# One PSUM tile for seven banks, and transposes without use in the tensor engine's early gaps

## The chip, the cores and the metric

The kernel runs on one core of a Trainium2 chip. The metric is the device time of one execution in microseconds (us); the time of before is the median of three executions. A profile is one execution recorded by the hardware profiler. Its engines are PE (the tensor engine's matmuls; PEld is its weight loads), DVE (the vector engine), ACT (the scalar engine), POOL (GpSimd) and SP (the queue that issues DMAs).

## The reference

Pre-layernorm attention with one key and value head, then a gated feed-forward layer, on 2048 tokens of width 512, all in fp32:

```python
def A(x, wq, wk, wv, wo):                      # 32 heads of 16, one k and one v
    q = (x @ wq).reshape(B, S, 32, 16).transpose(0, 2, 1, 3)
    p = softmax(einsum("bhqd,bkd->bhqk", q, x @ wk) * 16 ** -0.5)
    return einsum("bhqk,bkd->bhqd", p, x @ wv)...reshape(B, S, 512) @ wo
def Bf(x, W_gate, W_up, W_down):               # width 512 -> 1792 -> 512
    gate, up = x @ W_gate, x @ W_up
    return (gate * (gate > 0) * up) @ W_down
h = x + A(layernorm(x), wq, wk, wv, wo)
out = h + Bf(layernorm(h), W_gate, W_up, W_down)
```

## The kernel before

Matrices are split into a rounded part and a rest (fp32r), and a product is three matmul passes. Attention is cut into 32 units of 2048 query rows by 32 key steps (STEPS). For each of two row halves of the array (rows 0 to 63 and 64 to 127, which can compute beside each other) a step has two kinds of work:

- a **max matmul** (`max_mm`, L619): 512 columns of scores into one PSUM bank, of which DVE takes the row maxima (L621, one TENSOR_REDUCE of 128x512);
- a **score matmul** (`score_mm`, L658): 512 columns of scores, turned so that keys are on the partitions, of which ACT takes the exponential into SBUF (L661).

Two score steps feed one **value block** (`value_block`, L674): four matmuls of 32 columns each into a PSUM bank of its own, named O. The projections and the feed-forward layer are **chains** (`Chain`): accumulations of many passes into one bank, cut into two halves, one for each row half of the array (L297); at the end of a chain ACT (L861, L867) or DVE (L893, L822) reads the bank.

PSUM has eight banks. One is O. The other seven, BANKS = B0 to B6, are handed out by `bank(tag)`: each call makes a new tile of 128x512 fp32 with the bank's name and one buffer, so the next writer of B3 is made to wait for the last reader of B3. The framework adds all waits by itself, from which instruction writes and reads which tile.

What stands after what on every engine is written out by hand: ORDER is a row of 11,274 letters, read one at a time. m and M are a max matmul (lower and upper row half), e and E a score matmul, g and G one pass of a chain's lower or upper half, O a value block, T a set of transposes. The planner only chooses the bank (the free one that it thinks is earliest) and places work that the letters don't name. The row has 2048 m and M, 2048 e and E, 6648 g and G, 512 O and 18 T. The 512 O stand in 336 runs: 214 of one O, 89 of two, and 33 of three to five. 204 runs follow directly on an m, M, e or E. The first O is the 335th letter; `on_` counts the value blocks done. The chains of the row end in 186 readings: 16 query groups, 16 residuals, 98 gate products and 56 partial down products. After the last letter, `run(feed(NT - 1, True))` computes the last tile's feed-forward layer with whole chains (L288).

Of the kernel before, what the change touches and what calls it, by code (L numbers as in the profile page):

```python
# [16 lines left out]
S, D, H, DH, F = 2048, 512, 32, 16, 1792  # L17
# [9 lines left out]
STEPS = NB * 2  # L27
NP = 10
BANKS = [f"B{i}" for i in range(7)]
# [8 lines left out]
PASS, LOAD, SEEN, CHANGE, VALUE, BACK, TURN = 230, 107, 425, 95, 882, 237, 214  # L38

EXP, EXP_FREE, RED, RED_FREE, COPY, ADD, FREE = 494, 650, 600, 740, 541, 600, 150  # L40
ROUND, DIFF, PRODUCT, SCALE, HOP, ISSUE = 640, 1290, 1150, 640, 2600, 600
APPLY, LANDING, ASKED, SPREAD, RAW_LAG = 705, 4700, 5500, 5600, 1500


A_AT, V_AT, P_AT, QUERIES_AT, KEYS_AT, LN_AT = 1800, 1500, 3900, 0, 0, (0, 3000, 2500)

# [110 lines left out]
def block_kernel(ctx: ExitStack, tc: tile.TileContext, x, wq, wkv, wo, wgu, wd, out):  # L157
    nc = tc.nc
    pool = lambda name, **kw: ctx.enter_context(tc.tile_pool(name=name, bufs=1, **kw))
    consts = pool("consts")  # L160
    sb = pool("sb")
    ps = pool("ps", space=PSUM)
# [3 lines left out]
    ident = consts.tile([128, 128], F32, name="ident")  # L166
# [7 lines left out]
    kaug = consts.tile([128, S], F32R, name="kaug")  # L174
# [11 lines left out]


    rota = {"n": 0, "tags": []}

    def bank(tag=None):  # L190
        if tag is None:
            tag = rota["tags"][rota["n"] % len(rota["tags"])]
            rota["n"] += 1
        return ps.tile([128, 512], F32, name=tag, bufs=1)


    clk = {"A": 0.0, "V": 0.0, "P": 0.0, "S": 0.0}
    state = {"on": False, "spare": False, "now": 0.0}
    later, stamp = [], {}
    count = iter(range(1 << 30))  # L200

    def on(engine, t, ns):

        clk[engine] = max(clk[engine], t) + ns
        return clk[engine]

    def at(t, fn):

        if state["on"]:
# [376 lines left out]
    qaug = {}  # L586
# [21 lines left out]

    mpart = {}

    def max_mm(m, ab, tag):

        v, i = divmod(m, STEPS)
        j, p, c = i // 8, i // 4 % 2, i % 4
        if v not in mpart:
            mpart[v] = sb.tile([128, 2, 2, 4, 4], F32, name="mpart", bufs=2)
        r = slice(64 * ab, 64 * ab + 62)
        b = bank(tag)
        nc.tensor.matmul(b, qaug[v][r, p, c * 128:(c + 1) * 128], kaug[r, j * 512:(j + 1) * 512],  # L619
                         start=True, stop=True)  # L620
        nc.vector.tensor_reduce(mpart[v][:, ab, p, c, j:j + 1], b, axis=AX.X, op=ALU.max)  # L621

    def max_finish(v):

        m = sb.tile([128, 2, 8], F32, name="mfin", bufs=2)
        nc.vector.tensor_reduce(m.rearrange("p a n -> p (a n)"), mpart.pop(v).rearrange("p a q c j -> p (a q c) j"),
                                axis=AX.X, op=ALU.max)

        ms = sb.tile([128, 2, 2, 8], F32, name="msplit", bufs=2)
        nc.vector.tensor_copy(ms[:, :, 0].bitcast(F32R), m)  # L630
        nc.vector.tensor_tensor(ms[:, :, 1], m, ms[:, :, 0], op=ALU.subtract)

        mt = sb.tile([128, 32], F32, name="mturned", bufs=2)
        nc.vector.transpose(mt, ms.rearrange("p a l n -> p (a l n)"))
        t = on("V", 0.0, 950) + FREE

        def written():
            nc.sync.dma_start(out=c_dram[v], in_=mt)

        def landed():  # L640
            for ab in range(2):
                nc.sync.dma_start(out=qaug[v][64 * ab + 62:64 * ab + 64].bitcast(F32)
                                  .rearrange("l q (c i j) -> l (q c) i j", i=4, j=32),
                                  in_=c_dram[v].rearrange("(i a l n) j -> a l n i j", i=4, a=2, l=2)[ab])
            stamp["rows", v] = t + 2 * HOP

        at(t, written)
        at(t + HOP, landed)

    probs = {}  # L650

    def score_mm(g, ab, tag):

        v, i = divmod(g, STEPS)
        kb, p = divmod(i, 2)
        r = slice(64 * ab, 64 * ab + 64)
        b = bank(tag)
        nc.tensor.matmul(b, kaug[r, kb * 128:(kb + 1) * 128], qaug[v][r, p, :], start=True, stop=True)  # L658
        if g not in probs:
            probs[g] = sb.tile([128, 2, T], F32, name="p", bufs=NP)  # L660
        nc.scalar.activation(probs[g][:, ab], b, AF.Exp, scale=DH ** -0.5)  # L661

    obank, osb = {}, {}

# [242 lines left out]
    N = len(UNITS) * STEPS  # L907
# [16 lines left out]
    warm = bank("O")  # L924
# [108 lines left out]
    lanes = [0.0, 0.0]  # L1033
    issued = 0.0
    bfree = {tag: 0.0 for tag in BANKS + ["O"]}
    bfree.update(B0=V_AT, B6=V_AT - 200)
    free = list(BANKS)
    ge, me, on_ = [0, 0], [0, 0], 0
    exps, oend, qtime = {}, {}, {0: QUERIES_AT}
    maxed, loaded = 0, 1  # L1040
# [2 lines left out]
    clk.update(A=A_AT, V=V_AT, P=P_AT, S=0.0)  # L1043
    stamp.update({("xnT", 0, k): 0.0 for k in range(KT)})
    stamp["key", 0], stamp["ln", 1] = KEYS_AT, LN_AT[0]
    end_o, end_t = None, False

    def normalise(t):
# [127 lines left out]
    while not done():  # L1176
# [33 lines left out]
        tag = next_bank() if free else None  # L1210
        starts = {}
        for k in range(2):
            g, w, c = ge[k], me[k], (low, high)[k]
            if g < N and ("rows", g // STEPS) in stamp and g - NP < 2 * on_ and tag:
                starts["eE"[k]] = place(k, max(stamp["rows", g // STEPS], bfree[tag]))
            if w < N and w // STEPS in qtime and w // STEPS <= maxed + 1 and tag and (
                    w >= STEPS or ("key", w // 8) in stamp):
                starts["mM"[k]] = place(k, max(qtime[w // STEPS], bfree[tag], stamp["key", w // 8] if w < STEPS else 0.0))
            if c is not None and (c.tag or tag):
                starts["gG"[k]] = place(k, max(c.t, 0.0 if c.tag else bfree[tag]) if c.i == 0 else 0.0)  # L1220
        top = max(lanes)
        if on_ < N // 2 and len(exps.get(2 * on_ + 1, ())) == 2:
            dep = max(max(exps[g].values()) for g in range(2 * on_, 2 * on_ + 2)) + FREE
# [26 lines left out]
        if any(x.ready() + CHANGE <= top and (x.ready() + 4000 < top or on_ == N // 2) for x in turns):  # L1250
            do_turns()
            continue
        letter = next(order)
        if letter == "T":
            if pending in turns:
                turns.remove(pending)
            for source in (fronts, feeds):
                if source.held is pending:
                    source.held = None
            turn_now(pending, tag, False, end_t)  # L1260
            continue
        kind, k = letter.upper(), int(letter.isupper())
        issued = s = starts[letter]
        end_t = False
        if kind != "O":
            end_o = None
        if kind == "O":
            value_block(on_)
            v, i = divmod(on_, NB)
            end_o = s + VALUE  # L1270
            lanes = [end_o + BACK] * 2
            issued = end_o - 400
# [80 lines left out]
```

## Time and profile before

| | |
|---|---|
| median of three executions | 1734.67 us (1733.37 to 1734.95) |
| the profiled execution | 1735.53 us, span 1733.8 us from its first to its last instruction |
| mean granted clock of PE | 0.994 |

The profile's page has the busy time of each engine, the chain of waits that ended last, and groups of instructions by line with their mean duration and the idle time before them. The view by time (timeline) lists start, duration, engine, line, operation and count; a bracket gives the idle time before an instruction and what ended it. The view by windows gives, for a stretch of time, its length, then busy time and number of instructions of PE, PEld, DVE, ACT and POOL, then the granted clock of PE (1.00 is full speed), the DMA share and GB/s. Instructions of PE are pipelined, so a busy PE is not one at its peak.

### The profile page before, as it was taken

The page shows a single profiled execution, that of the slowest core. Times are in us where ns is not written, and L with a number is a line of the kernel's source. Part 1 is how long each engine was busy: PE and PEld are TensorE (multiplying, and loading weights), DVE is VectorE, ACT ScalarE, POOL GpSimd, SP SyncE. Part 2 cuts the span into 40 slices and gives each one's busy share as a digit, 9 for nine tenths or more (in the row PEclk, how much of TensorE's full clock was granted, in tenths as well). Part 3 has the DMA queues.
Part 4 walks back from the last instruction along what each step waited for, and adds up shares of the span by engine and source line. Part 5 has one row for each costly group of instructions (what it writes and reads, how often), then busy time and mean ns, then how long its engine had stood idle before and what let it go on. Part 6 is the DMA issues. An engine that isn't in the chain of part 4 may idle for free.

```text
span 1733.8 us, 40138 instructions
## 1 busy us (share of the span) xinstructions
PE 1712.0 (99%) x15566; PEld 1141.9 (66%) x15566; DVE 1451.0 (84%) x2524; ACT 1251.2 (72%) x2488; POOL 854.0 (49%) x1015
## 2 busy tenths in 40 slices
PE   8999999999999999999999999999999999999999
PEld 6755334766656666666766667666666666666688
DVE  8899999988998888988888888897898888986266
ACT  7478977777777777777777777777767777778724
POOL 5511301666415656286544667276655557276410
PEclk9999999999999999999999999999999999999999
DMA  3323211332212222233222223232223223122343
GB/s 129 92 74 86 77 32 26 97 95 79 83 58 72 75 79 81 71 96 97 77 61 83 77 87 99 72 103 70 79 69 108 77 79 102 48 87 81 107 138 116
DMA packets 101970, 144.07 MB, mean 83 GB/s; under 512 B 27156, under 2 KB 39572, under 8 KB 101780
## 3 DMA queue, kind: packets, MB, share of 16 engines
q1 hardware_dynamic: 100724, 141.19, 27.4%
q8 instruction: 122, 2.00, 0.5%
q14 instruction: 68, 0.56, 0.1%
q10 hardware_dynamic: 1056, 0.33, 0.1%
HBM read 119.73 MB, written 21.49 MB: 81 GB/s over the span
## 4 chain that ended last, share of the span: by engine, by line
PE 93%; DVE 5%; issue 1%; DMA 1%; ACT 0%; POOL 0%; SPq 0%; POOLq 0%; DVEq 0%; ACTq 0%
PE B L297 27%; PE O L674 27%; PE B L658 16%; PE B L619 16%; PE B L288 4%; DVE mpart L621 4%; PE B L514 1%; PE O L926 1%; PE B L404 0%; DVE msplit L630 0%; PE B L1001 0%; DMA c_dram<-mturned 0%; DVE hn L397 0%; DMA qaug<-c_dram 0%; PE B L581 0%
## 5 line engine op out<-in xcount | busy, mean ns | idle before, releaser
L621 DVE TENSOR_REDUCE mpart<-B 128x1 f32<-128x512 f32 x2048 | 1268.8, 682 | 190.6 <-PE B L619 111.6
L661 ACT ACTIVATE p<-B 128x512 f32<-128x512 f32 x2048 | 1091.0, 606 | 359.8 <-PE B L658 200.3
L619 PE MATMUL B<-kaug,qaug 62*128 62x512 f32 x2048 | 746.6, 421 | 8.3 <-DVE hT L566 2.6
L658 PE MATMUL B<-qaug,kaug 64*128 64x512 f32 x2048 | 713.6, 417 | 5.6 <-DMA qaug<-c_dram 3.6
L297 PE MATMUL B<-hn,gu 64*128 64x256 f32 x4704 | 564.8, 282 | 0.0
L297 PEld LDWEIGHTS B<-hn,gu 64*128 64x128 f32 x4704 | 533.9, 186 | 24.6 <-issue 15.6
L674 PE MATMUL O<-p,vv 128*32 128x512 f32 x4096 | 510.4, 601 | 0.0
L619 PEld LDWEIGHTS B<-kaug,qaug 62*128 62x128 f32 x2048 | 348.3, 185 | 157.7 <-DVE mpart L621 52.7
L658 PEld LDWEIGHTS B<-qaug,kaug 64*128 64x128 f32 x2048 | 337.6, 186 | 164.7 <-DVE mpart L621 53.4
L869 POOL TENSOR_TENSOR hf<-hf,ga 128x256 f32<-128x256 f32 x92 | 67.4, 733 | 426.0 <-ACT hf L867 417.7
L297 PE MATMUL B<-wd,hT 64*128 64x512 f32 x1176 | 274.6, 395 | 0.1
L240 POOL TENSOR_TENSOR gu<-wraw,gu 128x512 fp32r<-128x512 f32 x195 | 252.9, 1297 | 16.3
L674 PEld LDWEIGHTS O<-p,vv 128*32 128x32 f32 x4096 | 99.8, 109 | 192.0 <-issue 175.5
L297 PEld LDWEIGHTS B<-wd,hT 64*128 64x128 f32 x1176 | 192.0, 185 | 15.3 <-issue 2.7
L240 POOL TENSOR_TENSOR wd<-wraw,wd 128x512 fp32r<-128x512 f32 x95 | 122.4, 1289 | 7.9
L239 POOL TENSOR_SCALAR gu<-wraw 128x512 fp32r<-128x512 f32 x195 | 120.8, 619 | 11.1 <-PE B L297 8.0
L297 PE MATMUL B<-wo,act 64*128 64x512 f32 x384 | 88.3, 394 | 0.1
L240 POOL TENSOR_TENSOR hT<-hf,hT 128x256 fp32r<-128x256 f32 x97 | 72.9, 752 | 8.1
L357 POOL TENSOR_TENSOR rs<-ve,nhalf 128x2 f32<-128x2 f32 (+1 forms) x13 | 10.2, 783 | 125.5 <-DVE nm L353 125.4
L861 ACT ACTIVATE ga<-B 128x256 f32<-128x256 f32 x112 | 43.5, 388 | 39.0 <-PE B L288 24.6
L297 PEld LDWEIGHTS B<-wo,act 64*128 64x128 f32 x384 | 62.6, 185 | 5.5 <-issue 1.7
L528 POOL TENSOR_TENSOR act<-raw,act 128x512 fp32r<-128x512 f32 x16 | 20.6, 1290 | 89.4 <-ACT raw L527 85.7
(134 smaller groups left out, 916.3 us busy)
## 6 DMA issues: line engine op xcount, KB each, us to landing
wraw<-wgu SPq DMA_DIRECT2D x224, 256.0 KB
wraw<-wd SPq DMA_DIRECT2D x112, 256.0 KB
q_dram<-act SPq DMA_DIRECT2D x32, 256.0 KB
qaug<-q_dram SPq DMA_DIRECT2D x62, 128.0 KB
o_dram<-osb SPq DMA_DIRECT2D x31, 256.0 KB
x<-x SPq DMA_DIRECT2D x16, 256.0 KB
out<-h SPq DMA_DIRECT2D x16, 256.0 KB
qaug<-q_dram SPq DMA_DIRECT2D x62, 64.0 KB
```

Source lines behind the costliest of these rows:

```text
L239: nc.gpsimd.tensor_scalar(dst[:, 0], src, 1.0, 0.0, op0=ALU.mult, op1=ALU.add)
L240: nc.gpsimd.tensor_tensor(dst[:, 1], src, dst[:, 0].bitcast(F32), op=ALU.subtract)
L288: nc.tensor.matmul(out(self.bank), l(a), r(b), start=i == 0, stop=i == len(self.ops) - 1)
L297: mm = nc.tensor.matmul(out(self.bank), l(a)[rows], r(b)[rows], start=opens and which == 0, stop=closes and which == 1)
L528: nc.gpsimd.tensor_tensor(qs[:, 1], q, qs[:, 0].bitcast(F32), op=ALU.subtract)
L619: nc.tensor.matmul(b, qaug[v][r, p, c * 128:(c + 1) * 128], kaug[r, j * 512:(j + 1) * 512], start=True, stop=True)
L621: nc.vector.tensor_reduce(mpart[v][:, ab, p, c, j:j + 1], b, axis=AX.X, op=ALU.max)
L658: nc.tensor.matmul(b, kaug[r, kb * 128:(kb + 1) * 128], qaug[v][r, p, :], start=True, stop=True)
L661: nc.scalar.activation(probs[g][:, ab], b, AF.Exp, scale=DH ** -0.5)
L674: nc.tensor.matmul(obank[v][32 * h:32 * h + 32], vv[:, kb, :], probs[g + p][:, ab], start=kb == 0, stop=kb == NB - 1)
L861: nc.scalar.activation(ga[:, :n], p[:, :n], AF.Relu)
L869: nc.gpsimd.tensor_tensor(hf[:, :n], hf[:, :n], ga[:, :n], op=ALU.mult)
```

## The change

Three things change. The other parts of the diff (the letters X, P and W, `max_mm` and `score_mm` with a pair of banks, POOL_ROWS) are not reached: the row of letters is the same and has none of them, and POOL_ROWS is 0.

```diff
+WARMERS = True
+    banks = ps.tile([128, len(BANKS), 512], F32, name="B", bufs=1)
     def bank(tag=None):
...
-        return ps.tile([128, 512], F32, name=tag, bufs=1)
+        return banks[:, BANKS.index(tag)] if tag in BANKS else ps.tile([128, 512], F32, name=tag, bufs=1)
...
         kind, k = letter.upper(), int(letter.isupper())
+        if on_ == 0 and WARMERS:
+            idle = starts[letter] - max(last_busy, max(lanes) - 6000.0)
+            if idle > 400:
+                warm = bank("O")
+                for _ in range(min(16, int((idle - 200) / 150))):
+                    nc.tensor.transpose(warm[:, :128], ident, ident)
+            last_busy = starts[letter] + PASS
```

First, the seven banks become seven slices of one tile, made once. Second, as long as no value block has been computed, a gap of over 400 ns that the planner expects ahead of a letter gets up to 16 transposes of the identity into bank O. Third, some lines move (L619 is L627 now, L658 is L683, L297 is L303, L674 is L702, L621 is L630, L661 is L687).

The instructions of PE, DVE, ACT and POOL stand in the same order as before, and each uses the same bank, but for the added transposes on PE: 111, in 12 groups. The waits differ. In the order as built, with the engines that a row waits for, PE in the middle of the program stands so before the change (B2 and so on are the bank, the number behind it the tile, qaug and kaug the queries and keys, p the exponentials, wd and hT a chain's operands; the last two rows are the halves of two chains):

```order
L674 MATMUL O_6091<-p_6568,vv_79 32x512 x2
L619 MATMUL B2_6640<-kaug_78,qaug0_75 128x512 [waits DVE_49]
L658 MATMUL B5_6643<-qaug1_76,kaug_78 128x512 [waits Activation_49]
L658 MATMUL B6_6647<-qaug1_76,kaug_78 128x512 [waits Activation_49]
L658 MATMUL B3_6650<-qaug1_76,kaug_78 128x512 [waits DVE_49]
L297 MATMUL B0_6654<-wd_5756,hT_5447 128x512 [waits DVE_49]
L297 MATMUL B1_6590<-wd_5756,hT_5447 128x512 [waits Activation_sequencer_49]
```

Each of these waits is for the last reader of the same bank, which stands several matmuls further up: the score matmul into B6 waits for the exponential that last read B6. The same place of PE with the change (B_87 is the one tile):

```order
L702 MATMUL O_5142<-p_5548,vv_79 32x512 x2
L627 MATMUL B_87<-kaug_78,qaug0_75 128x512
L683 MATMUL B_87<-qaug1_76,kaug_78 128x512 [waits DVE_49]
L683 MATMUL B_87<-qaug1_76,kaug_78 128x512 [waits Activation_49] x2
L303 MATMUL B_87<-wd_4861,hT_4602 128x512 [waits Activation_49]
L303 MATMUL B_87<-wd_4861,hT_4602 128x512 [waits Activation_sequencer_49]
```

No instruction moved; the waits did. The count of the semaphore that each waits for belongs here to the reader of the matmul in the row directly above: the first score matmul waits for the reduction of the max matmul above it, the second for the exponential of the first, the third for that of the second, and the chain's pass for that of the third, though all four write different banks. Over the whole program PE's instructions have 2215 waits for ACT and 2177 for DVE before, 2198 and 2168 with the change. Before, nearly all are for a reader of the bank that is about to be written. With the change, 4351 of the 4366 are for the youngest reader of the tile that stands earlier in the program, whichever bank it reads.

DVE and ACT get waits too: DVE has 104 for ACT before and 1152 now, ACT 36 for DVE before and 940 now. Nearly all name a count that PE has already waited for ahead of the matmul whose result is to be read.

At the start of PE's row, ahead of the first value block, this stood (L581 are transposes of normalised inputs):

```order
L581 MATMUL B1_435<-ident_68,h_89 128x128 [waits Activation_49]
L581 MATMUL B1_435<-ident_68,h_90 128x128 [waits Pool_49] x2
L619 MATMUL B2_442<-kaug_78,qaug0_75 128x512 [waits DVE_49]
L581 MATMUL B3_445<-ident_68,h_89 128x128 [waits PE_49]
L581 MATMUL B3_445<-ident_68,h_89 128x128
```

and now the same place has three added transposes, and the same kind of waits as above:

```order
L587 MATMUL B_87<-ident_68,h_90 128x128 [waits Activation_49]
L587 MATMUL B_87<-ident_68,h_91 128x128 [waits Pool_49] x2
L1314 MATMUL O_433<-ident_68 128x128 [waits PE_49]
L1314 MATMUL O_433<-ident_68 128x128 x2
L627 MATMUL B_87<-kaug_78,qaug0_75 128x512 [waits Activation_49]
L587 MATMUL B_87<-ident_68,h_90 128x128 [waits DVE_49]
L587 MATMUL B_87<-ident_68,h_90 128x128
```

The transposes went in between; the max matmul now waits for ACT's reading of another bank, and the transposes behind it for the max matmul's reduction.

More of the change, by code (lines that the diff above doesn't have):

```diff
@@ L40 @@
 EXP, EXP_FREE, RED, RED_FREE, COPY, ADD, FREE = 494, 650, 600, 740, 541, 600, 150
+EXP_TWO, RED_TWO = 860, 1134
+ROWS_HOP, ROWS_AT = 2600, 5200
+POOL_ROWS = 0
+WARMERS = True
 ROUND, DIFF, PRODUCT, SCALE, HOP, ISSUE = 640, 1290, 1150, 640, 2600, 600
@@ L609, in block_kernel, with max_mm @@
     mpart = {}
-    def max_mm(m, ab, tag):
+    def max_mm(m, ab, tag, pair=None):
         v, i = divmod(m, STEPS)
@@ L616, in max_mm @@
             mpart[v] = sb.tile([128, 2, 2, 4, 4], F32, name="mpart", bufs=2)
[L617 to L621, printed above, removed]
+        for h in (ab, 1 - ab) if pair is not None else (ab,):
+            r = slice(64 * h, 64 * h + 62)
+            b = bank(tag) if pair is None else banks[:, pair + h]
+            nc.tensor.matmul(b, qaug[v][r, p, c * 128:(c + 1) * 128], kaug[r, j * 512:(j + 1) * 512],
+                             start=True, stop=True)
@@ L623, in max_finish @@
+        if pair is None:
+            nc.vector.tensor_reduce(mpart[v][:, ab, p, c, j:j + 1], b, axis=AX.X, op=ALU.max)
+        else:
+            nc.vector.tensor_reduce(mpart[v][:, :, p, c, j], banks[:, pair:pair + 2], axis=AX.X, op=ALU.max)
     def max_finish(v):
         m = sb.tile([128, 2, 8], F32, name="mfin", bufs=2)
-        nc.vector.tensor_reduce(m.rearrange("p a n -> p (a n)"), mpart.pop(v).rearrange("p a q c j -> p (a q c) j"),
-                                axis=AX.X, op=ALU.max)
@@ L629, in max_finish @@
         ms = sb.tile([128, 2, 2, 8], F32, name="msplit", bufs=2)
-        nc.vector.tensor_copy(ms[:, :, 0].bitcast(F32R), m)
-        nc.vector.tensor_tensor(ms[:, :, 1], m, ms[:, :, 0], op=ALU.subtract)
+        part = mpart.pop(v).rearrange("p a q c j -> p (a q c) j")
+        flat = m.rearrange("p a n -> p (a n)")
+        if v < POOL_ROWS:
+            half = sb.tile([128, 16, 2], F32, name="mhalf", bufs=2)
+            nc.gpsimd.tensor_tensor(half, part[:, :, :2], part[:, :, 2:], op=ALU.max)
+            nc.gpsimd.tensor_tensor(flat, half[:, :, 0], half[:, :, 1], op=ALU.max)
+            nc.gpsimd.tensor_scalar(ms[:, :, 0].bitcast(F32R), m, 1.0, None, op0=ALU.mult)
+            nc.gpsimd.tensor_tensor(ms[:, :, 1], m, ms[:, :, 0], op=ALU.subtract)
+            t = on("P", clk["V"] + FREE, 1000) + FREE
+            at(t, lambda: max_turned(v, ms, on("V", t, 250) + FREE))
+        else:
+            nc.vector.tensor_reduce(flat, part, axis=AX.X, op=ALU.max)
+            nc.vector.tensor_copy(ms[:, :, 0].bitcast(F32R), m)
+            nc.vector.tensor_tensor(ms[:, :, 1], m, ms[:, :, 0], op=ALU.subtract)
+            max_turned(v, ms, on("V", 0.0, 950) + FREE)
@@ L633, in max_finish, with max_turned @@
+    def max_turned(v, ms, t):
         mt = sb.tile([128, 32], F32, name="mturned", bufs=2)
         nc.vector.transpose(mt, ms.rearrange("p a l n -> p (a l n)"))
-        t = on("V", 0.0, 950) + FREE
         def written():
@@ L644, in landed, with score_mm @@
                                   in_=c_dram[v].rearrange("(i a l n) j -> a l n i j", i=4, a=2, l=2)[ab])
-            stamp["rows", v] = t + 2 * HOP
+            stamp["rows", v] = t + ROWS_AT
         at(t, written)
-        at(t + HOP, landed)
+        at(t + ROWS_HOP, landed)
     probs = {}
-    def score_mm(g, ab, tag):
+    def score_mm(g, ab, tag, pair=None):
         v, i = divmod(g, STEPS)
         kb, p = divmod(i, 2)
-        r = slice(64 * ab, 64 * ab + 64)
-        b = bank(tag)
-        nc.tensor.matmul(b, kaug[r, kb * 128:(kb + 1) * 128], qaug[v][r, p, :], start=True, stop=True)
+        for h in (ab, 1 - ab) if pair is not None else (ab,):
+            r = slice(64 * h, 64 * h + 64)
+            b = bank(tag) if pair is None else banks[:, pair + h]
+            nc.tensor.matmul(b, kaug[r, kb * 128:(kb + 1) * 128], qaug[v][r, p, :], start=True, stop=True)
         if g not in probs:
             probs[g] = sb.tile([128, 2, T], F32, name="p", bufs=NP)
-        nc.scalar.activation(probs[g][:, ab], b, AF.Exp, scale=DH ** -0.5)
+        if pair is None:
+            nc.scalar.activation(probs[g][:, ab], b, AF.Exp, scale=DH ** -0.5)
+        else:
+            nc.scalar.activation(probs[g], banks[:, pair:pair + 2], AF.Exp, scale=DH ** -0.5)
     obank, osb = {}, {}
@@ L1045, in block_kernel @@
     stamp["key", 0], stamp["ln", 1] = KEYS_AT, LN_AT[0]
+    last_busy = 0.0
     end_o, end_t = None, False
@@ L1220, in block_kernel @@
                 starts["gG"[k]] = place(k, max(c.t, 0.0 if c.tag else bfree[tag]) if c.i == 0 else 0.0)
+        pair = min((i for i in range(len(BANKS) - 1) if BANKS[i] in free and BANKS[i + 1] in free),
+                   key=lambda i: max(bfree[BANKS[i]], bfree[BANKS[i + 1]]), default=None)
+        ahead = int(lanes[0] > lanes[1])
+        if pair is not None:
+            both = max(bfree[BANKS[pair]], bfree[BANKS[pair + 1]])
+            g, w = ge[0], me[0]
+            if ge[0] == ge[1] and g < N and ("rows", g // STEPS) in stamp and g - NP < 2 * on_:
+                starts["X"] = place(ahead, max(stamp["rows", g // STEPS], both))
+            if me[0] == me[1] and w < N and w // STEPS in qtime and w // STEPS <= maxed + 1 and (
+                    w >= STEPS or ("key", w // 8) in stamp):
+                starts["P"] = place(ahead, max(qtime[w // STEPS], both, stamp["key", w // 8] if w < STEPS else 0.0))
         top = max(lanes)
@@ L1253, in block_kernel @@
         letter = next(order)
+        if letter == "W":
+            lanes = [max(l, later[0][0]) for l in lanes]
+            continue
         if letter == "T":
@@ L1262, in block_kernel @@
         kind, k = letter.upper(), int(letter.isupper())
+        if on_ == 0 and WARMERS:
[5 more added lines that the diff above has]
+            last_busy = starts[letter] + PASS
+        if kind in "XP":
+            s = starts[letter]
+            issued = max(lanes[1 - ahead], s)
+            lanes[ahead], lanes[1 - ahead] = s + PASS, issued + PASS
+            end_o, end_t = None, False
+            if kind == "X":
+                score_mm(ge[0], ahead, None, pair)
+                e0 = max(clk["A"], issued + SEEN, oend.get(ge[0] - NP, 0.0))
+                clk["A"] = e0 + EXP_TWO
+                exps[ge[0]] = {0: clk["A"] + 100, 1: clk["A"] + 100}
+                ge = [ge[0] + 1] * 2
+                done_at = e0 + EXP_TWO + 156
+            else:
+                max_mm(me[0], ahead, None, pair)
+                r0 = max(clk["V"], issued + SEEN)
+                clk["V"] = r0 + RED_TWO
+                me = [me[0] + 1] * 2
+                done_at = r0 + RED_TWO + 140
+                if me[0] == (maxed + 1) * STEPS:
+                    max_finish(maxed)
+                    maxed += 1
+            bfree[BANKS[pair]] = bfree[BANKS[pair + 1]] = done_at
+            continue
         issued = s = starts[letter]
```

## The prediction

> **What bounds the kernel now.** I read the page first: span, busy engines, chain of waits.
>
> ```profile
> span 1733.8 us, 40138 instructions
> PE 1712.0 (99%) x15566; PEld 1141.9 (66%) x15566; DVE 1451.0 (84%) x2524; ACT 1251.2 (72%) x2488; POOL 854.0 (49%) x1015
> PE 93%; DVE 5%; issue 1%; DMA 1%; ACT 0%; POOL 0%; SPq 0%; POOLq 0%; DVEq 0%; ACTq 0%
> ```
>
> PE is the bound: 99% busy, and 93% of the chain that ended last. DVE and ACT work beside it. The groups of instructions say what each does:
>
> ```profile
> L621 DVE TENSOR_REDUCE mpart<-B 128x1 f32<-128x512 f32 x2048 | 1268.8, 682 | 190.6 <-PE B L619 111.6
> L661 ACT ACTIVATE p<-B 128x512 f32<-128x512 f32 x2048 | 1091.0, 606 | 359.8 <-PE B L658 200.3
> L619 PE MATMUL B<-kaug,qaug 62*128 62x512 f32 x2048 | 746.6, 421 | 8.3 <-DVE hT L566 2.6
> L658 PE MATMUL B<-qaug,kaug 64*128 64x512 f32 x2048 | 713.6, 417 | 5.6 <-DMA qaug<-c_dram 3.6
> L297 PE MATMUL B<-hn,gu 64*128 64x256 f32 x4704 | 564.8, 282 | 0.0
> L926 PE MATMUL O<-ident 128*128 128x128 f32 x58 | 9.0, 334 | 1.3 <-POOL nhalf L169 1.3
> ```
>
> A max matmul is read by a reduction of 682 ns, a score matmul by an exponential of 606 ns; with seven banks, PE fills others meanwhile. The view of waits shows how seldom PE stands for a reader today:
>
> ```profile
> PEld B L658 <- DVE mpart L621: 53.4, 79, 2.3
> PEld B L619 <- DVE mpart L621: 52.7, 75, 2.0
> PEld B L658 <- ACT p L661: 51.6, 73, 0.8
> ```
>
> 79, 75 and 73 times, of 4096 such matmuls (columns: us in all, times, longest).
>
> **What the change does to that.** In the order as built, each matmul or chain pass that follows a max or score matmul waits for that matmul's own reader, though it writes another bank. So seven banks work like one: PE computes, the reader reads, PE goes on. The step from one m, M, e or E to the next instruction on the tile becomes matmul start to reader start, plus reader start to next matmul. The trace has both parts, where an engine stood idle and waited for just that. At full clock (a count covers a run of instructions from the first one's start):
>
> ```profile
> 38.23 0.73 PE L619 MATMUL B<-kaug,qaug 62*128 62x512 f32 x2
> 38.76 1.29 DVE L621 TENSOR_REDUCE mpart<-B 128x1 f32<-128x512 f32 x2 [2.85 <-PE B L619]
> 27.45 1.88 DVE L621 TENSOR_REDUCE mpart<-B 128x1 f32<-128x512 f32 x3
> 28.19 1.33 PE L619 MATMUL B<-kaug,qaug 62*128 62x512 f32 x3 [1.72 <-DVE mpart L621]
> 1640.12 0.50 PE L658 MATMUL B<-qaug,kaug 64*128 64x512 f32 x1
> 1640.66 0.60 ACT L661 ACTIVATE p<-B 128x512 f32<-128x512 f32 x1 [0.16 <-PE B L658]
> 1641.31 0.26 PEld L674 LDWEIGHTS O<-p,vv 128*32 128x32 f32 x6 [0.18 <-ACT p L661]
> ```
>
> Max matmul: 38.76 - 38.23 = 0.53, and 28.19 - 27.45 = 0.74 from the reduction's start to the matmul that it releases: 1.27 us. Score matmul: 0.54 + 0.65 = 1.19 us.
>
> **The clock.** PE would then stand still most of the time, and the granted clock falls when it does. The windows below go from one step of the clock to the next (busy PE is the second number, the clock the one behind POOL):
>
> ```profile
> 26.95:30.36 3.41, 1.50 (x4) 0.66 (x4) 3.41 (x6) 2.95 (x9) 1.45 (x3) 1.00 0.01 2
> 30.36:33.77 3.41, 1.53 (x6) 0.68 (x5) 3.41 (x7) 3.35 (x9) 1.20 (x2) 0.50 0.01 2
> 255.64:259.05 3.41, 1.49 (x5) 0.78 (x5) 3.41 (x7) 0.00 (x0) 0.00 (x0) 1.00 0.26 86
> 259.05:262.46 3.41, 3.18 (x13) 1.56 (x15) 2.03 (x5) 3.34 (x7) 0.00 (x0) 0.50 0.05 4
> 262.46:265.88 3.42, 3.42 (x19) 1.20 (x14) 2.05 (x5) 1.48 (x4) 0.00 (x0) 0.50 0.70 172
> 265.88:269.29 3.41, 3.36 (x26) 1.20 (x25) 2.56 (x6) 3.14 (x7) 1.28 (x1) 1.00 0.55 138
> ```
>
> Two windows with PE 44% busy (four and five matmuls) were followed by a clock of 0.50. A window at 0.50 with PE 93% busy (13 matmuls) did not bring the full clock back; one without a gap did. In the serial program a full-clock step has one matmul of about 0.5 us in 1.2 us, some 40% busy, which is where the clock fell; at half clock it is about 0.75 in 1.45, far below the 93% that didn't suffice. So I take half clock as the rule. Its prices:
>
> ```profile
> 261.97 1.93 PE L674 MATMUL O<-p,vv 128*32 128x512 f32 x8
> 263.83 0.80 PE L619 MATMUL B<-kaug,qaug 62*128 62x512 f32 x2
> 264.43 1.05 PE L658 MATMUL B<-qaug,kaug 64*128 64x512 f32 x3
> 264.66 1.89 DVE L621 TENSOR_REDUCE mpart<-B 128x1 f32<-128x512 f32 x3 [1.37 <-PE B L619]
> 265.09 2.06 ACT L661 ACTIVATE p<-B 128x512 f32<-128x512 f32 x4 [1.94 <-PE B L658]
> 265.83 1.07 PE L674 MATMUL O<-p,vv 128*32 128x512 f32 x8
> 266.83 0.50 PE L658 MATMUL B<-qaug,kaug 64*128 64x512 f32 x1
> ```
>
> Max matmul to reduction 264.66 - 263.83 = 0.83, with a switch after a value block in it; score matmul to exponential 265.09 - 264.43 = 0.66, with its weights loaded ahead, which a waiting matmul can't have. The slower start is bounded by 0.12 (0.66 - 0.54) and 0.30 (0.83 - 0.53). I take 0.78 and 0.72, inside both. The readers' own parts, 0.74 and 0.65, don't hang on PE's clock. Steps: 1.52 and 1.37 us.
>
> The Trainium skill ("TensorE: Matmul & The Clock Gate", Part 1: The HAM clock gate) says that the clock halves after an idle window of about 3.4 us. By that rule a matmul every 1.2 us would keep the clock full, and the time would be that of the full-clock rival below. The trace speaks against the strict reading: the window from 255.64 had five matmuls in it, and the clock still fell. The same page's section on psum-queue depth-cycling tells of a kernel whose short idles between groups of matmuls made the clock swing, which is the rival of a swinging clock.
>
> **The sum.** Counts come from the row of letters; the first figure is at half clock, the second at full.
> - Steps: 2048 x (1.52 + 1.37) = 5919 us; 2048 x (1.27 + 1.19) = 5038.
> - Value blocks: from one's start to the next instruction 263.83 - 261.97 = 1.86 and 266.83 - 265.83 = 1.00; 512 give 952 and 512. They write O, so the 204 behind a step's matmul run while its reader reads and save the rest of the step, about 1.0 each: 748 and 308.
> - Chain passes: these two rows are whole-chain passes of 256 and 512 columns.
>
> ```profile
> 1689.82 2.43 PE L288 MATMUL B<-hn,gu 128*128 128x256 f32 x19
> 1684.21 5.77 PE L288 MATMUL B<-wd,hT 128*128 128x512 f32 x24
> L661 ACTq EVENT_SEMAPHORE  x573: 17/17/17, 102.5 to 1634.8; - x191
> ```
>
>   2.43/19 = 0.128 and 5.77/24 = 0.24; over 4704 narrow and 1944 wide halves the mean is 0.161, double at half clock. Of 6648 halves, 3185 stand in the way of the next step on their own row half, counted along the row; the rest run beside the other half. 3185 x 0.32 = 1020; x 0.161 = 513.
> - Readers at 186 chain ends now hold PE as well: about 0.8 to the reader and 0.7 of it at half clock, 0.5 and 0.7 at full: 279; 223.
> - Ends: up to the first steps 28 us, after the last score matmul 1733.8 - 1640.1 = 94, and some 34 transposing turns and whole chains that wait a microsecond each: 175; 150.
> - Added transposes: 111 x 9.0/58 = 0.155 us is 17 us of PE. They fall where PE would stand waiting for a reader anyway: nothing taken, bound 17. Their gain in before's early gaps, a full instead of a half clock, is gone too, since a dozen groups can't keep warm what waits after each matmul.
> - Added waits of DVE and ACT for one another: they name counts that PE already had. Some 1600 more semaphore instructions at 17 ns: 28 us at most, inside the bounds.
> - Moved past other queues: nothing; SP and POOL keep their order. Weights and queries arrive at the same rate against a program over four times as long, so DMAs hide.
>
> Half clock: 8141 us. Full clock: 6232. At half clock, 33 runs of three to five value blocks (5.6 us and more) fill a window as the one from 262.46 did and bring one or two windows of full clock each, 170 us; with the start, the last 94 us and some runs of two, 330 us at full clock, which saves 330 x 8141/6232 - 330 = 101. The forecast is **8040 us**, 4.6 times before. The profiled execution took 1735.53 us, 1.7 over its span and 0.9 over the median of 1734.67, which is nothing against the terms here. The bounds of the two starts (0.65 to 0.83 and 0.66 to 0.84) make the steps 2048 x 2.70 = 5530 to 2048 x 3.06 = 6267, and the whole 7650 to 8390.
>
> **Rivals.**
> 1. *The clock swings.* If the half-clock program, busier by its longer matmuls, brings the clock back for a third to two thirds of the time, it ends between 6232 + (8141 - 6232)/3 = 6870 and 7500. For it: value blocks are dense. Against: the window of 93%.
> 2. *The clock stays full*: 6232, 6000 to 6700 with the same bounds. For it: at full clock the value blocks and passes add to the 40% of a step. Against: the windows of 44%.
> 3. *The waits cost nothing, the other side.* If every wait named a count long reached, PE would go on as before, 99% busy; the added transposes would then shorten the half clock from 30.36, saving at most half of two windows, 3.4 us: 1731. It decides where the matmul's wait is for a reader at least one step older than the one above it, since 0.74 us of reading fits in other matmuls. The order as built shows the youngest reader, which hasn't started. The Trainium skill ("PSUM — Partial Sum Buffer", PSUM bank collisions raise a hardware error) asks for guards by bank and quadrant only, so the chip doesn't need these waits; it obeys them all the same.
>
> **Chances.** Half clock (7650 to 8400) 0.66, slower still 0.05, swinging clock 0.19, full clock 0.08, no cost 0.02. The range 7100 to 8400 leaves out the full clock (0.08), the lower end of the swinging clock (0.05), the slower and the costless case (0.07): 0.2 in all. Within 0.2%, about what a measurement here can tell from no change, 0.005; faster 0.015; slower 0.98.
>
> **What would show it.** PE busy below 60% of the span; in the waits PE or PEld behind DVE mpart and ACT p over 3500 times, nearly a microsecond each; reductions and exponentials as often and as long as before, with DVE and ACT idle before almost each; PEclk near 0.5 in most slices; the chain of waits split over PE, DVE and ACT. A PEclk near 1.0 makes it rival 2. Wrong altogether if exponentials still follow each other without a gap.

## The result, and the profile after

The changed kernel takes 8113.43 us (median of 4 runs, 8109.92 to 8113.87) against 1734.02 for the kernel before on the same chip (4 runs, 1732.52 to 1734.95): 4.679 times as long, 95% interval 4.671 to 4.687. The profiled execution took 8113.5 us. The page of the kernel after, in the order in which the one before was read (span, busy engines, granted clock by slices, engines in the chain of waits):

```profile
span 8111.7 us, 42102 instructions
PE 4925.9 (61%) x15677; PEld 2145.0 (26%) x15677; DVE 1604.9 (20%) x2524; ACT 1406.6 (17%) x2488; POOL 845.5 (10%) x1015
...
PEclk6555555555555555555555555555555555555557
...
PE 61%; DVE 18%; ACT 16%; issue 4%; DVEq 0%; ACTq 0%; DMA 0%; POOL 0%; POOLq 0%
```

No engine is the bound any more. PE is busy 61% of the span, and no less than that only because a matmul at half clock lasts longer. The chain that ended last runs over all three engines in turn. The groups of instructions:

```profile
L683 PE MATMUL B<-qaug,kaug 64*128 64x512 f32 x2048 | 1541.6, 753 | 621.8 <-DVE mpart L630 364.8
L303 PE MATMUL B<-hn,gu 64*128 64x256 f32 x4704 | 1496.0, 482 | 1315.9 <-DVE mpart L630 670.7
L627 PE MATMUL B<-kaug,qaug 62*128 62x512 f32 x2048 | 1488.5, 727 | 450.7 <-ACT p L687 217.7
L630 DVE TENSOR_REDUCE mpart<-B 128x1 f32<-128x512 f32 x2048 | 1416.1, 691 | 6031.4 <-PE B L627 5969.4
L687 ACT ACTIVATE p<-B 128x512 f32<-128x512 f32 x2048 | 1223.2, 597 | 5982.2 <-PE B L683 5960.1
```

The readers are as many and as long as before (691 ns against 682, 597 against 606), while both their engines now stand idle for about 6000 us ahead of them. The matmuls went from 421 and 417 ns to 727 and 753, the chain passes from 282 to 482. The view of waits (engine and line, whom it waits for, us in all, times, longest):

```profile
DVE mpart L630 <- PE B L627: 5969.4, 2015, 12.6
ACT p L687 <- PE B L683: 5960.1, 2030, 13.3
...
PEld B L303 <- DVE mpart L630: 1511.8, 1170, 1.7
PEld B L303 <- ACT p L687: 1417.6, 1263, 1.5
PE B L303 <- DVE mpart L630: 1028.0, 1218, 1.3
PE B L303 <- ACT p L687: 947.4, 1345, 1.1
...
PEld B L683 <- DVE mpart L630: 603.1, 459, 1.9
...
PEld B L627 <- ACT p L687: 374.6, 314, 1.5
...
PEld B L683 <- ACT p L687: 369.0, 311, 2.0
...
PEld B L627 <- DVE mpart L630: 305.5, 239, 1.7
```

PE's weight loads wait 3756 times for a reduction or an exponential, 4582 us in all, where the three rows shown of before had 227 and a fourth (L619 behind an exponential) 45. And 2015 of 2048 reductions wait for their own matmul, 2030 of 2048 exponentials too: PE waits for the reader, the reader for PE. The timeline in the middle of the program shows one step after the other:

```profile
3006.46 0.79 PE L627 MATMUL B<-kaug,qaug 62*128 62x512 f32 x1
3007.37 0.69 DVE L630 TENSOR_REDUCE mpart<-B 128x1 f32<-128x512 f32 x1 [4.40 <-PE B L627]
...
3008.12 0.79 PE L683 MATMUL B<-qaug,kaug 64*128 64x512 f32 x1
3008.95 0.60 ACT L687 ACTIVATE p<-B 128x512 f32<-128x512 f32 x1 [2.54 <-PE B L683]
...
3009.60 1.22 PE L303 MATMUL B<-wd,hT 64*128 64x512 f32 x3 [0.69 <-ACT p L687]
...
3010.20 0.62 PE L627 MATMUL B<-kaug,qaug 62*128 62x512 f32 x1
3010.93 0.69 DVE L630 TENSOR_REDUCE mpart<-B 128x1 f32<-128x512 f32 x1 [2.88 <-PE B L627]
```

The max matmul of 3006.46 is read from 3007.37 on (0.91), and only 0.75 after that, at 3008.12, the score matmul starts, which goes to another bank. Its exponential starts 0.83 later, and 0.65 after that PE goes on: steps of 1.66 and 1.48 us. The rows left out here have weight loads and one chain pass that starts beside each of the first two matmuls. No second result is on its way to a reader while one is being read.

### The profile page after: what moved, and what is told of

It reads as the page before. It is cut to its first block, busy times and chain, and to the rows that moved or that the text cites. A ratio compares the mean times of both kernels' runs of the same rounds, so it can differ in the third digit from the quotient of the medians.

```text
span 8111.7 us, 42102 instructions
## 1 busy us (share of the span) xinstructions
PE 4925.9 (61%) x15677; PEld 2145.0 (26%) x15677; DVE 1604.9 (20%) x2524; ACT 1406.6 (17%) x2488; POOL 845.5 (10%) x1015
## 4 chain that ended last, share of the span: by engine, by line
PE 61%; DVE 18%; ACT 16%; issue 4%; DVEq 0%; ACTq 0%; DMA 0%; POOL 0%; POOLq 0%
PE B L303 25%; DVE mpart L630 17%; ACT p L687 15%; PE B L683 12%; PE B L627 11%; PE O L702 11%; PE B L294 1%; DVE h L921 1%; ACT ga L889 0%; ACT hf L895 0%; DVEq L630 0%; PE B L520 0%; PE B L410 0%; PE O L1314 0%; PE B L587 0%
## 5 line engine op out<-in xcount | busy, mean ns | idle before, releaser
L630 DVE TENSOR_REDUCE mpart<-B 128x1 f32<-128x512 f32 x2048 | 1416.1, 691 | 6031.4 <-PE B L627 5969.4
L303 PE MATMUL B<-hn,gu 64*128 64x256 f32 x4704 | 1496.0, 482 | 1315.9 <-DVE mpart L630 670.7
L687 ACT ACTIVATE p<-B 128x512 f32<-128x512 f32 x2048 | 1223.2, 597 | 5982.2 <-PE B L683 5960.1
L683 PE MATMUL B<-qaug,kaug 64*128 64x512 f32 x2048 | 1541.6, 753 | 621.8 <-DVE mpart L630 364.8
L627 PE MATMUL B<-kaug,qaug 62*128 62x512 f32 x2048 | 1488.5, 727 | 450.7 <-ACT p L687 217.7
L303 PEld LDWEIGHTS B<-hn,gu 64*128 64x128 f32 x4704 | 968.8, 304 | 1985.9 <-DVE mpart L630 946.3
L303 PE MATMUL B<-wd,hT 64*128 64x512 f32 x1176 | 669.2, 721 | 471.8 <-ACT p L687 238.5
L683 PEld LDWEIGHTS B<-qaug,kaug 64*128 64x128 f32 x2048 | 577.3, 282 | 1271.0 <-DVE mpart L630 603.1
L702 PE MATMUL O<-p,vv 128*32 128x512 f32 x4096 | 911.2, 1020 | 0.0
L627 PEld LDWEIGHTS B<-kaug,qaug 62*128 62x128 f32 x2048 | 592.8, 289 | 978.5 <-ACT p L687 374.6
L303 PEld LDWEIGHTS B<-wd,hT 64*128 64x128 f32 x1176 | 267.9, 290 | 813.6 <-ACT p L687 351.8
L303 PE MATMUL B<-wo,act 64*128 64x512 f32 x384 | 210.5, 701 | 151.0 <-ACT p L687 70.9
L702 PEld LDWEIGHTS O<-p,vv 128*32 128x32 f32 x4096 | 133.7, 150 | 345.1 <-issue 344.9
L303 PEld LDWEIGHTS B<-wo,act 64*128 64x128 f32 x384 | 85.0, 280 | 266.0 <-ACT p L687 121.9
L303 PE MATMUL B<-gu,wd 64*128 64x512 f32 x96 | 50.8, 755 | 41.9 <-ACT p L687 19.5
```

The lines of the kernel that those rows point to most:

```text
L303: mm = nc.tensor.matmul(out(self.bank), l(a)[rows], r(b)[rows], start=opens and which == 0, stop=closes and which == 1)
L702: nc.tensor.matmul(obank[v][32 * h:32 * h + 32], vv[:, kb, :], probs[g + p][:, ab], start=kb == 0, stop=kb == NB - 1)
```

## The experiments

The theory: the one tile, and nothing else in the change, makes every write to a bank wait for the youngest reader of any bank; the half clock is a consequence of the standing still and makes up the rest; the transposes matter little. The rivals: that making the tile once, rather than anew at each call, or slicing it is to blame; that the transposes are; that the loss is mainly the clock.

### The seven banks as tiles of their own again, transposes kept

```diff
-    banks = ps.tile([128, len(BANKS), 512], F32, name="B", bufs=1)
...
-        return banks[:, BANKS.index(tag)] if tag in BANKS else ps.tile([128, 512], F32, name=tag, bufs=1)
+        return ps.tile([128, 512], F32, name=tag, bufs=1)
```

> The changed kernel with one thing undone: each bank is again a tile of its own, made anew at each call; the 111 transposes and all else stay. Theory (the one tile makes each matmul wait for the youngest reader): all of the loss goes, 1728 to 1736 us, with the early half-clock stretch shortened by at most 3.4 us; exponentials back to back again, PE 99% busy. Rival (the transposes or another line of the change cause the loss): still above 8000 us. Rival (half and half): anything between.

Measured: 1744.87 us (5 runs, 1742.91 to 1745.72) against 1733.87, ratio 1.0063, 95% interval 1.0049 to 1.0076. Of the 6379 us lost all but 11 come back. Its view of waits has the kind of row that before had, not the one of after:

```profile
PEld B L682 <- DVE mpart L629: 54.1, 82, 2.4
```

So the tile is the cause of the loss. But the 11 us are a miss: the transposes by themselves cost something, where I had expected nothing or a small gain. The last three experiments look for it.

### Seven tiles of one bank each, made once and sliced

```diff
+    groups = [ps.tile([128, 1, 512], F32, name="Ba", bufs=1), ...]   # Ba to Bg
...
+        if tag in BANKS:
+            t, i = slots[BANKS.index(tag)]
+            return groups[t][:, i]
```

> As the changed kernel, but seven tiles of one bank each, all made once at the start and used again and again, so that only the sharing of a tile is gone and not its making once. Theory (waits follow the tile): 1728 to 1736 us, as with tiles made anew. Rival (a tile that is made once is what loses the knowledge of which reader is meant): about 8100 us.

Measured: 1742.89 us in one run, as the one above. Making a tile once, or handing out slices of it, costs nothing; that several banks share a tile does.

### Two tiles (four and three banks), and four (two, two, two, one)

The edit is the one above with other sizes, `[128, 4, 512]` and `[128, 3, 512]`, and `[128, 2, 512]` three times with one `[128, 1, 512]`.

> The changed kernel with the seven banks as two tiles, of four and three banks. In the order as built, 2693 waits are now for the youngest reader of all and 1217 for an older one, against 4351 for the youngest of the one tile. Theory (the wait is for the youngest reader of the same tile): about 1650 steps get free or nearly free, each 1.2 to 1.4 us, so 5800 to 6200 us, clock still near half. Rival (any tile that is shared costs the whole): about 8100 us. Rival (two independent halves, so half the time): about 4050 us.

> The changed kernel with the seven banks as four tiles: three of two banks, one of one. In the order as built 1089 waits are for the youngest reader of all, 712 for the one before it, 1208 for older ones. Theory: 8113 less about 2900 steps of 1.3 us, 4000 to 4600 us; the clock is back at full for a part of the time. Rival (any tile that is shared costs the whole): about 8100 us.

Measured: 6210.67 us with two tiles, clock 0.553, just above what I had expected; 4193.15 with four, clock 0.656, inside it. The busy engines of the two kernels:

```profile
PE 4237.7 (68%) x15677; PEld 1951.1 (31%) x15677; DVE 1592.9 (26%) x2524; ACT 1387.4 (22%) x2488; POOL 847.2 (14%) x1015
```
```profile
PE 3228.2 (77%) x15677; PEld 1651.4 (39%) x15677; DVE 1565.1 (37%) x2524; ACT 1354.8 (32%) x2488; POOL 850.1 (20%) x1015
```

With one, two, four and seven tiles the time is 8113, 6211, 4193 and 1743 us: it falls with the number of results that can be on their way at once. A write still waits for the youngest reader of its own tile, whichever bank that read. In the built order of two tiles 2693 waits of PE are for the youngest reader in the program, in that of four 1089, against 4351 with one tile.

### The one tile without the transposes

```diff
-WARMERS = True
+WARMERS = False
```

> The changed kernel without the 111 added transposes, still one tile. Theory: they hide in waits, 8090 to 8120 us, within 0.3% of the changed kernel. Rival (they matter in the serial program, by keeping the clock full at its start): 8140 us or more.

Measured: 8110.79 us in one run, 2.6 below the median of after and inside its runs. In the one-tile kernel the transposes fall where PE stands waiting, and cost nothing that can be told.

### The one tile with work that keeps the clock

Six transposes of the identity behind each max and score matmul, into an eighth bank that nobody reads; the row's banks are six slices of the one tile.

```diff
+FILL = 6
+    idle_bank = ps.tile([128, 512], F32, name="W", bufs=1)
+    def fill():
+        for _ in range(FILL):
+            nc.tensor.transpose(idle_bank[:, :128], ident, ident)
...
             nc.tensor.matmul(b, qaug[v][r, p, c * 128:(c + 1) * 128], ...)
+        fill()
```

> The changed kernel, still one tile and serial, with PE kept busy while it waits: six transposes of the identity into a bank that nobody reads stand behind each max and score matmul. For that bank the tile has six slices, and chains and steps are laid out over those six. Each transpose takes about 0.11 us at full clock, so 0.66 us fit into a wait of about 1 us. Theory (the clock is half because PE stands still): the clock returns to 1.00, steps are 1.27 and 1.19 us, and the time is 6232 us by the sum for full clock, up to 6700 where the transposes delay a matmul. Rival (the clock is no matter, the waits are all): above 8100 us, longer by what the transposes add.

Measured: 6563.49 us, clock 0.988. The group of the transposes, then the timeline at the place shown for after:

```profile
L201 PE MATMUL W<-ident 128*128 128x128 f32 x24576 | 3611.1, 284 | 0.0
```
```profile
3008.22 0.50 PE L647 MATMUL B<-kaug,qaug 62*128 62x512 f32 x1
3008.64 0.87 PE L201 MATMUL W<-ident 128*128 128x128 f32 x6
3008.75 0.69 DVE L651 TENSOR_REDUCE mpart<-B 128x1 f32<-128x512 f32 x1 [0.59 <-PE B L647]
3009.49 0.62 PE L323 MATMUL B<-hn,gu 64*128 64x256 f32 x3
```

Here the step is 0.53 + 0.74 = 1.27 us, exactly the full-clock step of the prediction. With 24,576 matmuls more the kernel is 1550 us faster than after: they run while PE would stand still, and bring back the clock. So of the 6379 us lost about 1550 are the clock (a lower bound, since the fill also delays what wouldn't have waited) and at most some 4830 the waits. It is 331 us above the prediction's full-clock sum of 6232. Some of that is seen: where nothing but fill stands between one step and the next, the steps take 1.29 and 1.23 us in the mean, against 1.27 and 1.19, which over 2048 of each is 133 us. Six transposes start 0.42 behind their matmul and take 0.87, so they end 1.29 behind it, later than the 1.19 at which the next matmul could start behind an exponential. The rest was not taken apart.

By the Trainium skill ("TensorE: Matmul & The Clock Gate", Part 4: PE-mode transpose), transposes don't engage the full clock as other matmuls do. This run speaks against that, with 0.988 against the 0.533 of the kernel without them; whether the framework's transposes ran in the mode that the page means, the trace doesn't tell.

### Reductions over half the columns, in both kernels

The row maximum is taken over 256 of the 512 columns, so the maxima of the other half are left out.

```diff
-            nc.vector.tensor_reduce(mpart[v][:, ab, p, c, j:j + 1], b, axis=AX.X, op=ALU.max)
+            nc.vector.tensor_reduce(mpart[v][:, ab, p, c, j:j + 1], b[:, :256], axis=AX.X, op=ALU.max)
```

> The changed kernel, where each reduction takes the maximum over the first 256 of its 512 columns (left out: the other half of the maxima). A DVE operation of 128x256 from PSUM takes 416 ns in the profile of before, a reduction of 128x512 682. Theory (the reader's whole duration lies on the path): 2048 x 0.27 = 550 us less, 7540 to 7590 us. Rival (DVE is 20% busy and hides): 8113 us.

> The kernel before with the same cut: each reduction over the first 256 of 512 columns (left out: the other half of the maxima). Theory: there the reduction lies beside PE's work, 0 to 40 us less, 1695 to 1735 us, though DVE is busy 84% there against 20% in the changed kernel. Rival (a reduction costs its duration in both): 550 us less, 1185 us.

Measured: 7587.15 us for the changed kernel, 526 less than 8113.43; for the kernel before 1719.23 against 1735.03 on the same chip, 16 less. The page of the first (DVE's busy time, the engines in the chain), then the reduction's group in the second:

```profile
PE 4909.8 (65%) x15677; PEld 2139.0 (28%) x15677; DVE 1058.3 (14%) x2524; ACT 1406.2 (19%) x2488; POOL 846.0 (11%) x1015
...
PE 60%; ACT 16%; issue 11%; DVE 11%; POOL 1%; DVEq 0%; ACTq 0%; DMA 0%; POOLq 0%
```
```profile
L621 DVE TENSOR_REDUCE mpart<-B 128x1 f32<-128x256 f32 x2048 | 812.6, 421 | 616.6 <-PE B L619 354.1
```

The same instruction got shorter by about the same amount in both (691 to 425 ns, and 682 to 421). DVE's busy time falls by 547 us in the changed kernel (1604.9 to 1058.3); 526 us, 96% of that, leave the span there, and 16 us with tiles of their own. This shows that a reading lies almost wholly on the path with the one tile, and hardly at all without.

### The own tiles with transposes in real gaps alone, and in the others alone

Where do the transposes cost 11 us? The rule for a gap subtracts 6000 ns from `max(lanes)`, the end of the work that the planner has already placed on PE, and `last_busy` is set by the letters alone. The sets of transposes (T) and whole chains placed between two letters thus count as a gap, though PE works. The timeline of the first experiment, and its window from 39 to 47 us:

```profile
39.01 1.91 PE L1313 MATMUL O<-ident 128*128 128x128 f32 x16
40.85 0.73 PE L626 MATMUL B<-kaug,qaug 62*128 62x512 f32 x2
41.51 1.97 PE L586 MATMUL B<-ident,p 128*128 128x128 f32 x16
43.80 1.97 PE L1313 MATMUL O<-ident 128*128 128x128 f32 x16
```
```profile
39.00:47.00 8.00, 8.00 (x64) 6.63 (x62) 4.75 (x7) 6.58 (x12) 2.97 (x2) 1.00 0.00 0
```

PE is busy for 8.00 of 8.00 us there, and two groups of 16 transposes take 1.9 us each. In the kernel before, which has none of them, PE is busy for 43.50 of the 44 us from 40 to 84, so there was hardly a gap for them. So I split the transposes by whether the gap is there without the 6000:

```diff
-            idle = starts[letter] - max(last_busy, max(lanes) - 6000.0)
+            idle = starts[letter] - max(last_busy, max(lanes))
```

leaves 20 transposes in two groups, at 25.8 and 32.3 us in the trace, and

```diff
-            if idle > 400:
+            if idle > 400 >= starts[letter] - max(last_busy, max(lanes)):
```

leaves the other 91 in ten groups. Both have own tiles.

> Own tiles again, and transposes only where the planner's own lanes have a gap: the idle time counts from the end of the last work of any kind, a set of transposes or a whole key chain too, instead of the last letter's step. 20 of the 111 transposes are left, in two groups, near 27 and 33 us. Theory (the other 91 stand behind work that the gap rule forgot, and cost their own length): the 11 us that own tiles with 111 transposes lost are back, and the clock stays full from 30 to 37 us: 1730 to 1734 us. Rival (any transposes there disturb what comes later): still about 1745 us.

> Own tiles, and only the 91 transposes that the kernel above leaves out, in ten groups. A group of 16 takes 1.9 us in the run with own tiles, 0.12 us each. Theory: 91 x 0.12 = 11 us more than before, 1742 to 1747 us. Rival (the two groups in the real gaps are what cost): about 1734 us.

Measured: with the 20 in real gaps 1734.64 us (11 runs, 1733.38 to 1736.74), ratio to before 1.0003, 95% interval 0.9994 to 1.0012, so no difference that can be told, and not the gain that the expected 1730 to 1734 allowed for; with the other 91 1743.05 (4 runs), ratio 1.0044 (1.0028 to 1.0059). The value blocks, in the order before, own tiles with all 111, with the 20, with the 91 (the two times are the starts of the first and the last):

```profile
L674 PE MATMUL O<-p,vv x4096: 592/593/1062, 93.0 to 1641.9; 128*32 128x512 f32 x196
```
```profile
L701 PE MATMUL O<-p,vv x4096: 592/592/1062, 100.2 to 1649.3; 128*32 128x512 f32 x196
```
```profile
L701 PE MATMUL O<-p,vv x4096: 592/592/1061, 92.7 to 1641.5; 128*32 128x512 f32 x196
```
```profile
L701 PE MATMUL O<-p,vv x4096: 592/592/1062, 101.7 to 1650.0; 128*32 128x512 f32 x196
```

The first value block is 7.2, -0.3 and 8.7 us later than before, the last one 7.4, -0.4 and 8.1. The loss arises ahead of the first value block, is carried almost unchanged to the end, and belongs to the 91 that stand where no gap is. The 20 in real gaps cost nothing, and win nothing either. The windows from 22 to 40 us of before and of the kernel with the 20:

```profile
22.00:40.00 18.00, 13.55 (x56) 8.67 (x55) 14.36 (x28) 13.90 (x30) 5.36 (x8) 0.81 0.00 1
```
```profile
22.00:40.00 18.00, 15.33 (x75) 10.49 (x75) 14.30 (x28) 13.73 (x30) 5.37 (x8) 0.91 0.00 1
```

The granted clock there rises from 0.81 to 0.91, and the first value block comes 0.3 us earlier. DVE and ACT are busy for 14 of the 18 us in both, so faster matmuls have little to gain there; what ends the waits between 40 and 93 us was not followed further. Of the kernels here that take all the maxima, none is faster than the one before.

## Why the prediction was right

**The mechanism.** Right. One tile makes each write wait for the youngest reader; the first two experiments show that it is the sharing, the two and four tiles that it goes by how many banks share, the half reductions that the reading is on the path.

**The clock.** Right: 0.533 over the span. At full clock were 529 us, summed from the clock's steps in the trace, not 330. Rival 1, a clock that swings for a third to two thirds of the time, is out at 6.5%; rival 2, the full clock, is what the fill made, 6563 (its bounds were 6000 to 6700). Rival 3, no cost, failed by its own condition: the waits are for the youngest reader. Its 1731 for the transposes alone was wrong as well: 1745.

**The sum**, 8040 against 8112 of span, hides larger misses. To size its terms, the 4095 intervals from one max or score matmul's start to the next one's were sorted by what PE did in between, from the starts in the trace:

| between two steps | intervals | mean us | sum us |
|---|---|---|---|
| nothing else | 1257 | 1.494 | 1878 |
| chain passes | 2492 | 1.855 | 4622 |
| value blocks | 181 | 3.115 | 564 |
| value blocks and passes | 144 | 5.096 | 734 |
| others (transposing turns, whole chains) | 21 | 6.63 | 139 |

The first step starts at 36.6 us, the last at 7973.7, 138.0 before the end. By these, with 1.494 as the price of a bare step:

- *Steps*: 4095 x 1.494 = 6118 us against 5919, 199 too low. The score matmul's start of 0.72 was the term mis-sized: in the 1257 bare steps it takes 0.80 in the mean, and the max matmul's 0.785, where the sum had 0.78. The readers' parts were right, 0.75 and 0.65, so the steps are 1.53 and 1.45 against 1.52 and 1.37. Over all pairs the starts take 0.83 and 0.81, inside the bounds given (0.65 to 0.83, 0.66 to 0.84) but at their top. The reason that I gave, that a waiting matmul can't have its weights loaded ahead, holds in 3008.12, where the start takes 0.83, but not always: the max matmul of 3010.20 stands behind chain passes, its weights were loaded from 3009.77 on, and its start takes 0.73. Of the max matmuls 31%, and of the score matmuls 18%, have a start below 0.76.
- *Chain passes and readers at chain ends*: 2492 x 0.361 + 144 x (5.096 - 3.115) = 1185 against 1020 + 279 = 1299, 114 too high.
- *Value blocks*, net of the full clock that they bring: 325 x (3.115 - 1.494) = 527 against 748 - 101 = 647, 120 too high; 529 us of full clock instead of 330 are part of that.
- *Ends*: 36.6 + 138.0 + 139 - 21 x 1.494 = 282 against 175, 107 too low. The sets of transposes and whole chains in the middle of the row cost more than a microsecond each.

199 - 114 - 120 + 107 = 72: that the sum came within 1% is partly that these cancel. The bounds held the time with room on both sides.

**Added transposes at nothing, bound 17.** Right in the kernel with the one tile (8110.8 without them, 8113.4 with). The reason given, that they fall where PE stands waiting for a reader, is all that hides them; with own tiles that cover is gone, and the 91 where no gap is cost 9 us (11 with all 111), of the bound of 17.

**Added waits of DVE and ACT for one another, 28 us at most.** No idle time shows them: of the 6031 us that DVE stood idle before its reductions 5969 ended with a max matmul, and of the 5982 us of ACT before its exponentials 5960 with a score matmul, and the two engines' queues (DVEq, ACTq) have 0% of the chain that ended last.

**What was to be seen.** PE busy below 60%: it was 61%, just missed, the longer matmuls being busier than thought. Over 3500 waits for the readers of nearly a microsecond each: 3756 of weight loads with a mean of 1.22, and the two rows of PE for L303 have 0.77. Readers as many and as long as before with idle ahead of almost each, PEclk at 5 in 38 of 40 slices, the chain split over three engines: as said.

## What to carry to other kernels

Where a framework derives waits from tiles, the tile and not the memory behind it is the unit of waiting: buffers that are to be in flight at once need tiles of their own, and the same slices that cost nothing one to a tile cost a factor of 4.7 seven to a tile. Before costing such a change, look in the built order at which reader each wait names, the youngest or one further up; from there the step is matmul start to reader start plus reader start to next matmul, both to be found in rows of the old trace. And filler goes only where the engine really stands still: a planner's gap that ignores part of the placed work puts it on the path.

## What the runs showed of the hardware

In the kernel after, the granted clock falls at one busy share of PE and comes back only at a higher one. Windows of 3.4 us of the kernel after, cut at the steps of the clock (PE's busy time is the second number, the clock the one behind POOL):

```profile
3038.15:3041.57 3.42, 1.85 (x4) 0.68 (x4) 1.78 (x4) 0.00 (x0) 0.00 (x0) 0.50 0.01 2
3041.57:3044.98 3.41, 3.41 (x17) 0.79 (x20) 0.39 (x2) 0.60 (x1) 0.00 (x0) 0.50 0.04 5
3044.98:3048.39 3.41, 2.22 (x15) 0.60 (x7) 0.39 (x1) 0.60 (x1) 0.00 (x0) 1.00 0.69 224
3048.39:3051.81 3.42, 1.51 (x6) 0.66 (x6) 0.99 (x2) 0.60 (x1) 0.00 (x0) 1.00 0.05 16
3051.81:3055.22 3.41, 1.60 (x6) 1.00 (x6) 0.89 (x2) 0.60 (x1) 0.00 (x0) 0.50 0.00 0
```

A gapless window at half clock brings the full clock; one with PE 65% busy keeps it; one with 44% and six matmuls loses it. Over the whole trace of after, 101 windows at full clock were followed by the half: PE was busy for a median of 44% of them, 60% at most; 54 were followed by another at full clock, with 56% at least. Of the 100 half-clock windows that brought the full clock back, 96 were 92% busy or more. The 2119 that stayed at half had a median of 55%, but 30 of them were as busy as 92% too. So a step of about 40% busy at full clock drops to half, and at half clock, where it is some 55% busy, it stays there: the serial program holds itself at the slow clock. These shares are no sharp thresholds: with four tiles the full clock fell behind windows up to 76% busy, and in the kernel with the fill up to 75%, so more than PE's busy share in this view decides, and what it is stays open. By the Trainium skill ("TensorE: Matmul & The Clock Gate", Part 1: The HAM clock gate) the clock halves after an idle window of about 3.4 us. The length of the window agrees with these rows, idle does not: a window with six matmuls is enough.
